# A Fourier filter feeding a snake MLP: the cosine's bias as an immediate, and the transform's pieces placed at other steps

## The chip, the cores and the metric

The kernel runs on one NeuronCore of a Trainium2 chip. The metric is the device time of one execution in microseconds. Five engines run side by side, each with a queue of its own that it works through in order: PE (TensorE, matmuls), ACT (ScalarE), DVE (VectorE), POOL (GpSimd, here only DMA loads that change the type) and SP (SyncE, here all other DMAs after the start).

## The reference

```python
# x (8, 3008, 256), filt_r and filt_i (1505, 256), w_in (256, 2048), w_out (2048, 256), alpha (2048)
X = np.fft.rfft(x, axis=1)
Y = X * (filt_r + 1j * filt_i)[None, :, :]
y = np.fft.irfft(Y, n=3008, axis=1).reshape(8 * 3008, 256)
h = y @ w_in
s = np.sin(alpha * h)
g = h + s * s / (alpha + 1e-09)
out = g @ w_out
```

## The kernel before

**The spectral part.** 3008 = 47 × 64, so each of the 8 batches goes through a transform in two factors and back, in three stages that `spectral(b)` cuts into pieces:

- Stage 1, 8 pieces: a matmul `pa` over the 47 (tile `x`, table `wf_t`), two per piece, evacuated into `t1`; after every second piece a chunk of `t1` is stored to the DRAM buffer `d1`. After the last piece eight loads bring `d1` back in another order as four `t2` tiles, two loads each.
- Stage 2, 13 pieces: piece u does the forward matmul `pb` over the 64 (two of them), its evacuation `xf` by ACT and two products `p` with the filter by DVE, and then, for u − 1, the inverse matmul `pc` (four of them) and its evacuation `g`. Every third one stores `g` to the DRAM buffer `d2` in two DMAs.
- Stage 3, 16 pieces: four small matmuls `pd` over the 47 on a chunk of `d2`, loaded as `t4` (four loads per batch, three buffers), and an evacuation into `y`. Two consecutive pieces fill the two halves of the channels for 376 columns of `y`. `y` holds two batches, even and odd.

`evac` (L135, L137) sends two evacuations in three to ACT and the third to DVE. All matmul results of the spectral part share the two PSUM slots of `fps`; only batch 0's `pb` uses `ops`.

**The MLP.** Two batches are 6016 columns, taken in 12 chunks of at most 512. A chunk is 8 steps. In each step `hidden` runs twice: two matmuls `ph` (L356) into one of the four slots of `hps`, the cosine `cos` by ACT (L359), and `v` = cos − 1 − ph by DVE (L360). With sin² written as a cosine of twice the angle, and alpha folded into the two weight matrices at the start, this is the snake function. Then `project` multiplies 128 columns of the chunk before by half of `w2` (eight matmuls `po`, L371); every fourth step ACT copies the result to `o` (L377) and SP stores it.

**The order.** Batch b's MLP begins at about step 48·b. The list `pending` holds the spectral pieces of batches 1 to 7, and of batch 0 what is left, by the step at which each is due; `plan` gives these steps for each stage. In a step the pieces that are due come after `hidden` and before `project`. This is the order in which the program is written; the tile framework's scheduler then orders every engine's queue by its own estimate of when operands and buffers are ready, with the written order as priority. The trace shows that loads leave earlier than written where their buffer is free.

**The start.** Batch 0's stages run before the MLP. Its loads, the filter's (`filt` into `f_t`, doubled onto the other 64 partitions by `dup_filter`), the inverse table `e_t` (from transposes of `d_t`) and the weights are chained by `after(ins, other)`, which makes a DMA wait for another instruction, and `behind`, which only keeps an order. `marks` keeps the latest instruction of a kind for that: `w_out` is loaded after `marks["t4"]`, and batch 1's `x` after the `marks["t4"]` of its moment.

Of the kernel before, what the change touches and what calls it, by code (L numbers as in the profile page):

```python
# [54 lines left out]
def kernel(  # L55
# [76 lines left out]
    def evac(dst, src, on_act=None):  # L132
        flip[0] = (flip[0] + 1) % 3
        if flip[0] if on_act is None else on_act:
            marks["act"] = nc.scalar.copy(out=dst, in_=src)  # L135
        else:
            marks["dve"] = nc.vector.tensor_copy(out=dst, in_=src)  # L137

    def spectral(b):

        pieces = []
        d1 = dpool.tile([2 * NS, N2, C], FP16, name=f"d1_{b}", tag="d1")
        d2 = dpool.tile([2 * NS, N2, C], FP16, name=f"d2_{b}", tag="d2")
        d1_rows = d1.rearrange("a (h n) c -> (a h) n c", h=2)
        d2_rows = d2.rearrange("a (h n) c -> (a h) n c", h=2)
        st = {}

        def stage1(u):
            ch, half = divmod(u, 2)
            if u == 0:  # L150
                st["x"] = load_x(b)
            if half == 0:
                st["t1"] = t1pool.tile([NK, 8, C], FP16, name=f"t1_{b}_{ch}", tag="t1")
            for i in range(2):
                n0 = 4 * half + 2 * i
                ps = fps.tile([128, 512], FP32, name=f"pa_{b}_{u}_{i}", tag="f")
                marks["pe"] = nc.tensor.matmul(out=ps[0:NK, :], lhsT=wf_t, rhs=st["x"][ch][:, n0:n0 + 2, :],  # L157
                                               start=True, stop=True)
                evac(st["t1"][:, n0:n0 + 2, :], ps[0:NK, :])
            if half == 1:  # L160
                nc.sync.dma_start(out=d1_rows[:, 8 * ch:8 * ch + 8, :], in_=st["t1"])
            if u == 7:
                st["t2"] = []
                for g in range(4):
                    t2 = t2pool.tile([128, 6, C], FP16, name=f"t2_{b}_{g}", tag="t2")
                    for p in range(2):
                        a0 = p * NS + 6 * g
                        eng = nc.scalar if b == 0 and p else nc.sync
                        marks["t2", g] = eng.dma_start(out=t2[64 * p:64 * p + 64, :, :],
                                          in_=d1[a0:a0 + 6, :, :].rearrange("s n c -> n s c"))  # L170
                    st["t2"].append(t2)

        def stage2(u):
            if u < 12:

                ps = (ops if b == 0 else fps).tile([128, 2, C], FP32, name=f"pb_{b}_{u}",
                                                   tag="o" if b == 0 else "f")
                for i in range(2):
                    s = 2 * u + i
                    nc.tensor.matmul(out=ps[:, i, :], lhsT=d_t[:, s, :],  # L180
                                     rhs=st["t2"][s // 6][:, s % 6, :], start=True, stop=True)
                xf = xfpool.tile([128, 2, C], FP16, name=f"xf_{b}_{u}", tag="xf")
                nc.scalar.copy(out=xf, in_=ps)  # L183
                pr = []
                for k in range(2):
                    pt = ppool.tile([128, 2, C], FP16, name=f"p_{b}_{u}_{k}", tag="p")
                    marks["prod", u] = nc.vector.tensor_tensor(out=pt, in0=xf, in1=f_t[k][:, 2 * u:2 * u + 2, :],  # L187
                                                               op=ALU.mult)
                    pr.append(pt)
                st["p", u] = pr  # L190
            if u > 0:
                w = u - 1
                pr = st.pop(("p", w))
                if w % 3 == 0:
                    st["g"] = gpool.tile([128, 6, C], FP16, name=f"g_{b}_{w}", tag="g")
                ps = fps.tile([128, 2, C], FP32, name=f"pc_{b}_{w}", tag="f")
                for i in range(2):
                    for k in range(2):
                        nc.tensor.matmul(out=ps[:, i, :], lhsT=e_t[:, k, 2 * w + i, :],  # L199
                                         rhs=pr[k][:, i, :], start=(k == 0), stop=(k == 1))  # L200
                i0 = 2 * (w % 3)
                evac(st["g"][:, i0:i0 + 2, :], ps, i0 != 2 if b == 0 else None)
                if w % 3 == 2:
                    for p in range(2):
                        a0 = p * NS + 6 * (w // 3)
                        nc.sync.dma_start(out=d2[a0:a0 + 6, :, :].rearrange("s n c -> n s c"),
                                          in_=st["g"][64 * p:64 * p + 64, :, :])

        def stage3(u):
            ch, rest = divmod(u, 4)  # L210
            half, cb = divmod(rest, 2)
            if rest == 0:
                t4 = t4pool.tile([NK, 8, C], FP16, name=f"t4_{b}_{ch}", tag="t4")
                marks["t4"] = nc.sync.dma_start(out=t4, in_=d2_rows[:, 8 * ch:8 * ch + 8, :])
                st["t4"] = t4
            ps = fps.tile([128, 4, 128], FP32, name=f"pd_{b}_{u}", tag="f")
            psv = ps.rearrange("p a b -> p (a b)")[:, 0:4 * NR].rearrange("p (a r) -> p a r", r=NR)
            for i in range(4):
                nc.tensor.matmul(out=psv[:, i, :],  # L219
                                 lhsT=st["t4"][:, 4 * half + i, cb * 128:cb * 128 + 128],  # L220
                                 rhs=wi_t, start=True, stop=True)
# [44 lines left out]

    def dup_filter(g):
        gs = slice(6 * g, 6 * g + 6)
        for k in range(2):
            ins = nc.vector.tensor_copy(out=f_t[k][64:128, gs, :], in_=f_t[k][0:64, gs, :])  # L270
            behind(ins, marks["prod", 3 * g - 2] if g else s1_dve)

    for g in range(4):
        for k, filt in enumerate((filt_r, filt_i)):
            for q in range(2):
                off, step = ((6 * g) * C, C) if q == 0 else ((N1 - 6 * g) * C, -C)
                ins = nc.gpsimd.dma_start(
                    out=f_t[k][32 * q:32 * q + 32, 6 * g:6 * g + 6, :],
                    in_=bass.AP(tensor=filt.tensor, offset=filt.offset + off,
                                ap=[[N1 * C, 32], [step, 6], [1, C]]))  # L280
                if g >= 2:
                    after(ins, marks["t2", g - 2])
    for g in range(3):
        pse = ops.tile([128, 8, 128], FP16, name=f"pse_{g}", tag="o")
        for i in range(8):
# [63 lines left out]
    def hidden(k, jb):  # L349
# [6 lines left out]
            nc.tensor.matmul(out=ps[:, 0:n], lhsT=w1[:, cb, jb * 128:jb * 128 + 128],  # L356
                             rhs=y_cols[:, cb, c0:c0 + n], start=(cb == 0), stop=(cb == 1))
        cs = cospool.tile([128, 512], FP32, name=f"cos_{k}_{jb}", tag="c")
        nc.scalar.activation(out=cs[:, 0:n], in_=ps[:, 0:n], func=AFT.Sin, bias=quarter)  # L359
# [21 lines left out]
    def store(o_blk, pb, col):  # L381

        p = 0
        while p < 128:
# [70 lines left out]
```

## Time and profile before

| | us |
|---|---|
| median of 10 runs | 841.02 (840.12 to 844.12) |
| profiled execution | 840.12, its span 838.3 |
| PE busy | 799.5 (95% of the span) |
| ACT busy | 674.9 (81%) |
| DVE busy | 628.6 (75%) |
| PE clock, mean granted | 0.985 |

Busy time is the time in which an engine has an instruction in work. Matmuls overlap, so a PE that is busy throughout can still stand between two of them. The first 60 us of the span are the start, in which PE is busy for about six tenths and the DMA engines carry the most; after it every slice has PE at nine tenths or more.

### The profile page before, as it was taken

To read this page: it belongs to the slowest core of one execution; us is meant where nothing else is said; L and a number is where in the kernel's file an instruction comes from. 1 tells how busy PE (TensorE), PEld (TensorE's weight loads), DVE (VectorE), ACT (ScalarE), POOL (GpSimd) and SP (SyncE) were. 2 spreads that over 40 slices of the span, in tenths; PEclk is the share of its full clock that TensorE was granted. 3 is DMA by queue.
4 is the path that set the end of the run, shared out by engine and by line. 5 is a ranking of instruction groups with operands and counts; after the bars stand their busy time and mean duration, and the time that the engine had idled before them with its cause. 6 is when DMAs were issued, how large, how long until landed. Compare 5 with 4: busy or idle time off the path is not lost.

```text
span 838.3 us, 16120 instructions
## 1 busy us (share of the span) xinstructions
PE 799.5 (95%) x5793; PEld 543.9 (65%) x5793; DVE 628.6 (75%) x1120; ACT 674.9 (81%) x1200; POOL 28.1 (3%) x55
## 2 busy tenths in 40 slices
PE   5758999999999999999999999999999999999996
PEld 2325676667776676666776677666767677666674
DVE  3658886778877787777877788777877778777772
ACT  4547897888878898888888888888988988788873
POOL 3210000000000000000000000000000000000000
PEclk9959999999999999999999999999999999999998
DMA  9985844285354833367242753447343343421111
GB/s 214 224 246 123 194 95 131 51 177 113 82 135 89 178 84 92 91 137 157 66 130 61 166 135 82 115 91 171 91 97 92 98 113 83 115 57 38 38 39 45
DMA packets 93495, 94.98 MB, mean 113 GB/s; under 512 B 8084, under 2 KB 82852, under 8 KB 93416
## 3 DMA queue, kind: packets, MB, share of 16 engines
q1 hardware_dynamic: 84784, 75.02, 34.6%
q0 software_dynamic: 6704, 18.09, 12.6%
q10 hardware_dynamic: 1928, 0.86, 0.5%
q8 instruction: 45, 0.74, 0.4%
q14 instruction: 34, 0.28, 0.1%
HBM read 58.02 MB, written 49.81 MB: 129 GB/s over the span
## 4 chain that ended last, share of the span: by engine, by line
PE 83%; DMA 6%; DVE 4%; ACT 4%; issue 2%; SPq 0%; ACTq 0%; DVEq 0%; POOLq 0%
PE ph L356 35%; PE po L371 35%; PE pc L199 5%; PE pa L157 4%; DMA t<-d 3%; PE pd L219 2%; PE pb L180 2%; ACT cos L359 2%; DMA w_out<-in_moe_w_out_dram 1%; DVE v L360 1%; DVE p L187 1%; DMA d<-t 1%; DMA d<-g 1%; ACT y L135 1%; DMA x<-in_x_dram 1%
## 5 line engine op out<-in xcount | busy, mean ns | idle before, releaser
L360 DVE SCALAR_TENSOR_TENSOR v<-cos,ph 128x512 f16<-128x512 f32 (+1 forms) x768 | 483.6, 671 | 147.9 <-ACT cos L359 146.9
L359 ACT ACTIVATE cos<-ph,quarter 128x512 f32<-128x512 f32 (+1 forms) x768 | 480.8, 680 | 104.9 <-PE ph L356 103.7
L371 PE MATMUL po<-w,v 128*128 128x256 f16 x3008 | 400.7, 273 | 2.7 <-DVE w L339 2.7
L356 PE MATMUL ph<-y,w 128*128 128x512 f16 (+1 forms) x1536 | 391.8, 377 | 0.2 <-ACT y L135 0.2
L371 PEld LDWEIGHTS <-v 128*128 128x128 f16 x3008 | 288.6, 98 | 79.1 <-issue 7.4
L356 PEld LDWEIGHTS <-w 128*128 128x128 f16 x1536 | 150.7, 98 | 102.8 <-issue 5.5
L187 DVE TENSOR_TENSOR p<-xf,filt 128x512 f16<-128x512 f16 x192 | 71.9, 417 | 5.9 <-ACT xf L183 5.2
L377 ACT COPY o<-po 128x512 f32<-128x512 f32 x96 | 56.5, 589 | 9.8 <-PE po L371 7.4
L183 ACT CAST xf<-pb 128x512 f16<-128x512 f32 x96 | 56.6, 590 | 8.9 <-DMA t<-d 5.5
L199 PE MATMUL pc<-p,e_t 128*128 128x256 f16 x384 | 60.1, 278 | 3.4 <-DVE p L187 2.1
L135 ACT CAST t<-pa 96x512 f16<-96x512 f32 x89 | 50.0, 588 | 15.0 <-PE pa L157 15.0
L219 PEld LDWEIGHTS <-t 96*128 96x128 f16 x512 | 35.7, 99 | 39.3 <-DMA t<-d 12.1
L157 PE MATMUL pa<-x,wf_t 94*96 94x512 f16 x128 | 47.6, 410 | 10.2 <-DMA x<-in_x_dram 6.2
L219 PE MATMUL pd<-wi_t,t 96*128 96x94 f16 x512 | 42.6, 208 | 10.6 <-DMA t<-d 9.9
L199 PEld LDWEIGHTS <-e_t 128*128 128x128 f16 x384 | 37.7, 99 | 16.3 <-issue 7.5
L135 ACT CAST y<-pd 128x376 f16<-128x376 f32 x82 | 38.7, 474 | 11.4 <-PE pd L219 11.4
L180 PE MATMUL pb<-t,d_t 128*128 128x256 f16 x192 | 37.8, 280 | 3.2 <-DMA t<-d 2.4
L135 ACT CAST g<-pc 128x512 f16<-128x512 f32 x64 | 38.7, 605 | 2.2 <-PE pc L199 1.9
L137 DVE CAST y<-pd 128x376 f16<-128x376 f32 x46 | 25.2, 548 | 19.3 <-PE pd L219 19.2
L137 DVE CAST t<-pa 96x512 f16<-96x512 f32 x39 | 26.7, 684 | 17.2 <-PE pa L157 16.6
L180 PEld LDWEIGHTS <-d_t 128*128 128x128 f16 x192 | 18.7, 100 | 24.9 <-DMA t<-d 3.7
L118 POOL DMA_DIRECT2D x<-in_x_dram x32 | 16.6, 522 | 503.6 <-PE pa L157 493.0
(29 smaller groups left out, 86.2 us busy)
## 6 DMA issues: line engine op xcount, KB each, us to landing
d<-t SPq DMA_DIRECT2D x32, 384.0 KB
d<-g SPq DMA_DIRECT2D x64, 192.0 KB
t<-d SPq DMA_DIRECT2D x32, 384.0 KB
x<-in_x_dram POOLq DMA_DIRECT2D x32, 376.0 KB, 7.3
t<-d SPq DMA_DIRECT2D x60, 192.0 KB
out_dram<-o SPq DMA_DIRECT2D x72, 94.0 KB
w_in<-in_moe_w_in_dram POOLq DMA_DIRECT2D x2, 1024.0 KB, 9.1
w_out<-in_moe_w_out_dram POOLq DMA_DIRECT2D x1, 2048.0 KB, 11.9
```

The source lines that it names most:

```text
L135: marks["act"] = nc.scalar.copy(out=dst, in_=src)
L157: marks["pe"] = nc.tensor.matmul(out=ps[0:NK, :], lhsT=wf_t, rhs=st["x"][ch][:, n0:n0 + 2, :], start=True, stop=True)
L180: nc.tensor.matmul(out=ps[:, i, :], lhsT=d_t[:, s, :], rhs=st["t2"][s // 6][:, s % 6, :], start=True, stop=True)
L183: nc.scalar.copy(out=xf, in_=ps)
L187: marks["prod", u] = nc.vector.tensor_tensor(out=pt, in0=xf, in1=f_t[k][:, 2 * u:2 * u + 2, :], op=ALU.mult)
L199: nc.tensor.matmul(out=ps[:, i, :], lhsT=e_t[:, k, 2 * w + i, :], rhs=pr[k][:, i, :], start=(k == 0), stop=(k == 1))
L219: nc.tensor.matmul(out=psv[:, i, :], lhsT=st["t4"][:, 4 * half + i, cb * 128:cb * 128 + 128], rhs=wi_t, start=True, stop=True)
L356: nc.tensor.matmul(out=ps[:, 0:n], lhsT=w1[:, cb, jb * 128:jb * 128 + 128], rhs=y_cols[:, cb, c0:c0 + n], start=(cb == 0), stop=(cb == 1))
L359: nc.scalar.activation(out=cs[:, 0:n], in_=ps[:, 0:n], func=AFT.Sin, bias=quarter)
L360: marks["snake"] = nc.vector.scalar_tensor_tensor(out=v[k][:, jb, 0:n], in0=cs[:, 0:n], scalar=-1.0, in1=ps[:, 0:n], op0=ALU.add, op1=ALU. ...
L371: nc.tensor.matmul(out=pso[k][:, t % 2, :], lhsT=v[k][:, jb, 128 * t:128 * t + 128], rhs=w2[:, jb, :], start=(jb == 0), stop=(jb == 15))
L377: nc.scalar.copy(out=o[:, 0:nb, :], in_=pso[k][:, 0:nb, :])
```

## The change

- `quarter`, a [128,1] tile filled with π/2, is dropped. The cosine takes the number itself as its bias.
- The list of due steps becomes the function `at_step`. With s = 48·b − 4·(b odd), for batches 2 to 7: the loads of `x` at s − 72 (before: with stage 1's first piece, at 48·b − 45), stage 1 at s − 50 to s − 43 (before: 48·b − 45 to − 38), stage 2 at s − 36 to s − 12 in every second step (before: 48·b − 29 to − 16, nearly one per step), stage 3 at s − 6, − 5, − 4, − 3, then − 1, 1, and so on to 21 (before: 48·b − 10, − 9, − 7, − 5, and so on to 19). Batch 1 has stage 1 at 6 to 13 and stage 2 at 21 to 33 (before: 8 to 15 and 23 to 35), and stage 3 by the rule above.
- For batches 2 to 7 `load_x` is a piece of its own, of a stage 0.
- Stage 3 loads `t4` one chunk ahead: chunks 0 and 1 at its first piece, then chunk 2 and chunk 3 at pieces 4 and 8.
- The signs of the second product are placed otherwise: `filt_i` is loaded onto the upper 64 partitions and its negative goes onto the lower ones, and both halves of `e_t[:, 1]` are negated copies. Stage 2 is cut into the functions `forward`, `product` and `inverse`, whose bodies are those of before.

```diff
         def stage1(u):
             ch, half = divmod(u, 2)
-            if u == 0:
+            if u == 0 and b < 2:
                 st["x"] = load_x(b)
...
         def stage2(u):
+
             if u < 12:
...
+                forward(u)
+                st["p", u] = [product(k, u) for k in range(2)]
             if u > 0:
...
+                inverse(u - 1)
+
+        def load_t4(ch):
+            st["t4", ch] = t4pool.tile([NK, 8, C], FP16, name=f"t4_{b}_{ch}", tag="t4")
+            marks["t4"] = nc.sync.dma_start(out=st["t4", ch], in_=d2_rows[:, 8 * ch:8 * ch + 8, :])
 
         def stage3(u):
...
             if rest == 0:
-                t4 = t4pool.tile([NK, 8, C], FP16, name=f"t4_{b}_{ch}", tag="t4")
-                marks["t4"] = nc.sync.dma_start(out=t4, in_=d2_rows[:, 8 * ch:8 * ch + 8, :])
-                st["t4"] = t4
+                for c in ([0, 1] if ch == 0 else [ch + 1] if ch < 3 else []):
+                    load_t4(c)
...
+        if b >= 2:
+            pieces.append((0, lambda: st.update(x=load_x(b))))
         for u in range(8):
             pieces.append((1, lambda u=u: stage1(u)))
...
-    quarter = cpool.tile([128, 1], FP32)
-    nc.vector.memset(quarter, float(np.pi / 2))
...
     def dup_filter(g):
         gs = slice(6 * g, 6 * g + 6)
-        for k in range(2):
-            ins = nc.vector.tensor_copy(out=f_t[k][64:128, gs, :], in_=f_t[k][0:64, gs, :])
+        for ins in (nc.vector.tensor_copy(out=f_t[0][64:128, gs, :], in_=f_t[0][0:64, gs, :]),
+                    nc.vector.tensor_scalar(out=f_t[1][0:64, gs, :], in0=f_t[1][64:128, gs, :],
+                                            scalar1=-1.0, scalar2=None, op0=ALU.mult)):
...
-                    out=f_t[k][32 * q:32 * q + 32, 6 * g:6 * g + 6, :],
+                    out=f_t[k][64 * k + 32 * q:64 * k + 32 * q + 32, 6 * g:6 * g + 6, :],
...
-        nc.vector.tensor_copy(out=e_t[0:64, 1, gs, :], in_=e_t[64:128, 0, gs, :])
-        nc.vector.tensor_scalar(out=e_t[64:128, 1, gs, :], in0=e_t[0:64, 0, gs, :],
-                                scalar1=-1.0, scalar2=None, op0=ALU.mult)
+        for p in range(2):
+            nc.vector.tensor_scalar(out=e_t[64 * p:64 * p + 64, 1, gs, :],
+                                    in0=e_t[64 - 64 * p:128 - 64 * p, 0, gs, :],
+                                    scalar1=-1.0, scalar2=None, op0=ALU.mult)
...
-        nc.scalar.activation(out=cs[:, 0:n], in_=ps[:, 0:n], func=AFT.Sin, bias=quarter)
+        nc.scalar.activation(out=cs[:, 0:n], in_=ps[:, 0:n], func=AFT.Sin, bias=float(np.pi / 2))
...
-    plan = {1: [-45 + i for i in range(8)],
-            2: [-29 + 14 * i / 13 for i in range(13)],
-            3: [-10, -9] + [-7 + 2 * i for i in range(14)]}
+    def at_step(b, stage, i):
+
+        if b == 1 and stage < 3:
+            return 6 + i if stage == 1 else 21 + i
+        return 48 * b - 4 * (b % 2) + (-72 if stage == 0 else -50 + i if stage == 1
+                                       else -36 + 24 * i / 12 if stage == 2
+                                       else -6 + i if i < 4 else -1 + 2 * (i - 4))
+
     pending = [(1 + i % 4 + 8 * (i // 4), 0, piece) for i, (_, piece) in enumerate(first[25:])]
     for b in range(1, B):
-        at = {1: 0, 2: 0, 3: 0}
+        at = {0: 0, 1: 0, 2: 0, 3: 0}
         for stage, piece in spectral(b):
-            at_step = 48 * b + plan[stage][at[stage]]
-            if b == 1 and stage < 3:
-                at_step = 8 + at[stage] if stage == 1 else 23 + at[stage]
+            pending.append((at_step(b, stage, at[stage]), b, piece))
             at[stage] += 1
-            pending.append((at_step, b, piece))
```

More of the change, by code (lines that the diff above doesn't have):

```diff
@@ L171, in stage1, with forward @@
                     st["t2"].append(t2)
+        def forward(u):
+            ps = (ops if b == 0 else fps).tile([128, 2, C], FP32, name=f"pb_{b}_{u}",
+                                               tag="o" if b == 0 else "f")
+            for i in range(2):
+                s = 2 * u + i
+                nc.tensor.matmul(out=ps[:, i, :], lhsT=d_t[:, s, :],
+                                 rhs=st["t2"][s // 6][:, s % 6, :], start=True, stop=True)
+            xf = xfpool.tile([128, 2, C], FP16, name=f"xf_{b}_{u}", tag="xf")
+            nc.scalar.copy(out=xf, in_=ps)
+            st["xf", u] = xf
@@ new lines, in product, with inverse @@
+        def product(k, u):
+            pt = ppool.tile([128, 2, C], FP16, name=f"p_{b}_{u}_{k}", tag="p")
+            marks["prod", u] = nc.vector.tensor_tensor(out=pt, in0=st["xf", u],
+                                                       in1=f_t[k][:, 2 * u:2 * u + 2, :], op=ALU.mult)
+            return pt
+        def inverse(w):
+            pr = st.pop(("p", w))
+            if w % 3 == 0:
+                st["g"] = gpool.tile([128, 6, C], FP16, name=f"g_{b}_{w}", tag="g")
+            ps = fps.tile([128, 2, C], FP32, name=f"pc_{b}_{w}", tag="f")
+            for i in range(2):
+                for k, pt in enumerate(pr):
+                    nc.tensor.matmul(out=ps[:, i, :], lhsT=e_t[:, k, 2 * w + i, :],
+                                     rhs=pt[:, i, :], start=(k == 0), stop=(k == len(pr) - 1))
+            i0 = 2 * (w % 3)
+            evac(st["g"][:, i0:i0 + 2, :], ps, i0 != 2 if b == 0 else None)
+            if w % 3 == 2:
+                for p in range(2):
+                    a0 = p * NS + 6 * (w // 3)
+                    nc.sync.dma_start(out=d2[a0:a0 + 6, :, :].rearrange("s n c -> n s c"),
+                                      in_=st["g"][64 * p:64 * p + 64, :, :])
@@ L173, in stage2 @@
         def stage2(u):
             if u < 12:
[L176 to L182, printed above, removed]
@@ L183, in stage2 @@
-                nc.scalar.copy(out=xf, in_=ps)
-                pr = []
-                for k in range(2):
[L186 to L190, printed above, removed]
-            if u > 0:
[L192 to L207, printed above, removed]
@@ L219, in stage3 @@
                 nc.tensor.matmul(out=psv[:, i, :],
-                                 lhsT=st["t4"][:, 4 * half + i, cb * 128:cb * 128 + 128],
+                                 lhsT=st["t4", ch][:, 4 * half + i, cb * 128:cb * 128 + 128],
                                  rhs=wi_t, start=True, stop=True)
@@ L268, in dup_filter @@
         gs = slice(6 * g, 6 * g + 6)
-        for k in range(2):
-            ins = nc.vector.tensor_copy(out=f_t[k][64:128, gs, :], in_=f_t[k][0:64, gs, :])
+        for ins in (nc.vector.tensor_copy(out=f_t[0][64:128, gs, :], in_=f_t[0][0:64, gs, :]),
+                    nc.vector.tensor_scalar(out=f_t[1][0:64, gs, :], in0=f_t[1][64:128, gs, :],
+                                            scalar1=-1.0, scalar2=None, op0=ALU.mult)):
             behind(ins, marks["prod", 3 * g - 2] if g else s1_dve)
@@ L289 @@
         behind(nc.scalar.mul(e_t[:, 0, gs, :], pse, 0.125), s1_act)
-        nc.vector.tensor_copy(out=e_t[0:64, 1, gs, :], in_=e_t[64:128, 0, gs, :])
-        nc.vector.tensor_scalar(out=e_t[64:128, 1, gs, :], in0=e_t[0:64, 0, gs, :],
-                                scalar1=-1.0, scalar2=None, op0=ALU.mult)
+        for p in range(2):
+            nc.vector.tensor_scalar(out=e_t[64 * p:64 * p + 64, 1, gs, :],
+                                    in0=e_t[64 - 64 * p:128 - 64 * p, 0, gs, :],
+                                    scalar1=-1.0, scalar2=None, op0=ALU.mult)
     ones = cpool.tile([128, 128], FP32)
```

## The prediction

> **What bounds the kernel now.** I read the page first: TensorE (PE) is busy 95% of the span and carries 83% of the chain that ended last. The cosine is the largest ScalarE (ACT) row, and it takes `quarter` as a second operand:
>
> ```profile
> PE 83%; DMA 6%; DVE 4%; ACT 4%; issue 2%; SPq 0%; ACTq 0%; DVEq 0%; POOLq 0%
> ...
> L359 ACT ACTIVATE cos<-ph,quarter 128x512 f32<-128x512 f32 (+1 forms) x768 | 480.8, 680 | 104.9 <-PE ph L356 103.7
> L371 PE MATMUL po<-w,v 128*128 128x256 f16 x3008 | 400.7, 273 | 2.7 <-DVE w L339 2.7
> L356 PE MATMUL ph<-y,w 128*128 128x512 f16 (+1 forms) x1536 | 391.8, 377 | 0.2 <-ACT y L135 0.2
> L377 ACT COPY o<-po 128x512 f32<-128x512 f32 x96 | 56.5, 589 | 9.8 <-PE po L371 7.4
> ```
>
> ACT waits 103.7 us for `ph`, while PE waits only 0.2 us for ACT at the hidden matmuls. So ACT's speed can pay only where PE waits for a PSUM slot that ACT or VectorE (DVE) empties. Busy time hides such waits, because matmul ends are modelled. I therefore took the part at full PE clock from the stage windows:
>
> ```profile
> 72.00:828.00 756.00, 751.51 (x5569) 519.27 (x5568) 588.74 (x1034) 640.55 (x1142) 12.32 (x24) 1.00 0.44 104
> ```
>
> (length; PE, weight loads, DVE, ACT, POOL busy with counts; PE clock, DMA share, GB/s). The same view by line gives the matmuls in it: 1508 `ph` (128 of them 384 wide by the code), 2972 `po`, 109 `pa`, 168 `pb`, 336 `pc`, 476 `pd`.
>
> **What the Trainium skill says.** "TensorE: Matmul & The Clock Gate", section "Wait — 56ns, not 53.3ns?": a warm matmul of N columns starts N/2.4 GHz + about 2.5 ns after the one before. The trace agrees: eight 256-wide `po` run at 0.87 us, 109 ns each. "ScalarE: Activation LUTs", section "What ACT_TABLE_LOAD costs": an ACTIVATE with immediates costs 186 ns + 0.833 ns per element, each [128,1] pointer about 93 ns more, and neighbours overlap by about 93 ns. The trace agrees closely: 680 ns for the cosine against 589 ns for the copy `o` of the same shape, which has no pointer. "VectorE: DVE Perf Modes", section "The perf-mode tier table": tensor_copy and tensor_scalar share a tier. Here the two 64x1024 f16 instructions on `e_t` took 422 and 420 ns.
>
> **The stalls there are to win.** Issue time of that window: 1380×215.8 + 128×162.5 + 2972×109.2 + 109×215.8 + 504×109.2 + 476×42.5 ns (42.5 is the measured pitch of `pd`) = 741.8 us of 756. So PE stands still for 14 us. Going through start-to-start distances and adding each excess over the matmul's own pitch gives 14.0 us: 5.9 before `pa` (stage 1), 4.8 before `pc` (stage 2), 2.3 before `pd` (stage 3), 0.7 before `ph`, 0.3 before `pb`. That is the ceiling: 1.7%. Two typical ones, from the timeline (start, length, engine, line, what):
>
> ```profile
> 367.60 1.26 ACT L359 ACTIVATE cos<-ph,quarter 128x512 f32<-128x512 f32 x2 [0.44 <-PE ph L356]
> ...
> 368.30 0.93 PE L371 MATMUL po<-w,v 128*128 128x256 f16 x7
> ...
> 368.75 0.47 ACT L135 CAST y<-pd 128x376 f16<-128x376 f32 x1
> ...
> 369.28 0.38 PE L157 MATMUL pa<-x,wf_t 94*96 94x512 f16 x1
> ...
> 402.77 0.68 DVE L137 CAST g<-pc 128x512 f16<-128x512 f32 x1
> ...
> 403.01 0.49 PE L371 MATMUL po<-w,v 128*128 128x256 f16 x3
> ...
> 403.50 0.60 PE L199 MATMUL pc<-p,e_t 128*128 128x256 f16 x4
> ```
>
> First: seven `po` from 368.30 are through at 369.07, but `pa` starts at 369.28, when ACT has emptied `y` out of one of the two `fps` slots. ACT came to `y` late because two cosines stood ahead. Second: three `po` end at 403.34, but `pc` waits until 403.50 for DVE's `g`, which stood behind two `v` and two products.
>
> **The change, part by part.**
>
> *Immediate bias.* 768 × about 92 ns = 71 us of ACT time, nearly all off the path. On the path is the queue ahead of an evacuation: two cosines, so 0.18 us sooner, against stalls of 0.05 to 0.3 us before `pa`. I take 3.0 of 5.9 us, with 1 and 5 as bounds: later units inherit the earlier finish, but where more stage-3 units meet stage 1 (below) less is won. The dropped memset is one small instruction at the start, nothing.
>
> *Stage 2 over 24 steps for batches 2 to 7.* The count stays at 13 pieces and 8 stores per batch. A piece every second step gives the two slots 4.1 us instead of 2.4 us, so DVE's `g` is out in time: the 4.1 us before `pc` in these batches go (bounds 2.5 and 4.5). Batch 1 keeps one per step and its 0.7.
>
> *Batch 1 two steps earlier.* Its stage 2 ends 5 steps ahead of stage 3, not 3. A 1.3 us stall before `pd` at 142.9 for `t4` (1.18 us in the waits view) should mostly go: 1.0 (0 to 1.3).
>
> *Stage 3 and `t4`.* Four loads per batch as before. Loading one chunk ahead gains nothing: the scheduler already sends the second and third early (237.19 and 237.56, one step after the first at 235.10). Starting with four units in a row puts 6 of the 8 stage-1 steps of batches 3, 5, 7 beside a stage-3 unit instead of 4: three evacuations through two slots. I charge 0.7 us (0 to 2). Consumers are at least one step later, as before.
>
> *`load_x` as a piece of its own.* POOL carries only loads by then, and each waits for `pa` to free its buffer (4 x tiles; the waits view has 493 us of it). An earlier place in the program changes no issue: 0.
>
> *Filter and `e_t` signs.* Copy becomes tensor_scalar, same counts: 0.
>
> *The price at the start.* `w_out` is released by `marks["t4"]`. Unit 0 now loads two chunks, so the mark is the second one:
>
> ```profile
> 48.28 1.26 SPq L214 DMA_DIRECT2D t<-d  x3
> ...
> 52.90 1.18 POOL L332 DMA_DIRECT2D w_out<-in_moe_w_out_dram  x1 [17.86 <-DMA t<-d]
> ...
> 64.78 1.14 DVE L339 TENSOR_SCALAR w<-w_out,rec_t 128x256 f16<-128x256 f32 x4 [3.35 <-DMA w_out<-in_moe_w_out_dram]
> ...
> 65.19 1.37 PE L371 MATMUL po<-w,v 128*128 128x256 f16 x7 [2.72 <-DVE w L339]
> ```
>
> Three `t4` loads leave SP together; the second lands about 1.6 us after the first (384 KB at the page's best slice, 246 GB/s). `w_out` takes 11.85 us in the chain and PE stands 2.72 us behind it, with DVE's `v` queued behind `w`. So it goes onto the path whole: 1.5 us lost (0 to 3; a further stretch at half clock would be the upper end). Batch 1's x loads now wait for the third `t4`, but POOL sends them after `w_out` anyway.
>
> *The price at the hand-over to stage 2.* From stage 1's last unit to stage 2's first there were 9 steps, now 7. Over 7 steps PE does 7×(4×215.8+8×109.2) + 2×215.8 + 16×42.5 ns = 13.3 us, and the data need: evacuation, `d1` store, `t2` loads.
>
> ```profile
> 470.48 0.60 PE L157 MATMUL pa<-x,wf_t 94*96 94x512 f16 x2
> ...
> 472.92 0.32 SPq L161 DMA_DIRECT2D d<-t  x1
> 474.56 4.29 SPq L389 DMA_DIRECT2D out_dram<-o  x4
> 481.39 5.28 SPq L169 DMA_DIRECT2D t<-d  x8
> ...
> 487.39 0.38 PE L180 MATMUL pb<-t,d_t 128*128 128x256 f16 x2
> ```
>
> That is batch 5: 10.9 us from `pa` to the first `t2` load. Batches 2, 3, 4, 6 took 8.0 to 9.0 us, batch 7 (no x prefetch beside it) 5.3. The first group is two loads; it lands 5.3 us after the first issue in batch 1 (0.65 + 4.64 in the chain). The need is thus 13.3 to 14.3 us, 16.2 in batch 5, against 13.3: 0 to 1 us late in most. By semaphore events other batches land nearer 4.5 us, and evacuations come sooner with the shorter cosine. I charge 2.0 us over six batches (0 to 7). SP has nothing of the batch queued between; output stores wait behind `t2`, with three `o` buffers as cover.
>
> **The sum.** Won: 3.0 + 4.1 + 1.0 = 8.1. Lost: 1.5 + 0.7 + 2.0 = 4.2. Net 3.9 us. The profiled execution took 840.12 us, of which 838.3 are its span; the median of the runs is 841.02, 0.9 above. 840.1 − 3.9 + 0.9 gives **837.0 us**. About 0.2% (1.7 us) is what a measurement of this kernel can tell from no change.
>
> **The rivals.**
>
> *Forecast*, chance 0.52: 833 to 839.2 us.
>
> *All cover holds*, 0.15: `t2` is in time, collisions cost nothing and the start loses nothing or reorders around it. Won 10 to 12, so 829 to 832. For it: batch 7's margin. Against it: the `w_out` chain is visible and has no spare work beside it.
>
> *The saving lands in idle time*, 0.14: ACT's 71 us only lengthen its wait for `ph`, or the immediate isn't decoded as one and the record stays at 680 ns. Stage 2's gain alone (4.1) is eaten by the same losses: 841, within 0.2%. For it: the 103.7 us that ACT already waits. Against it: stalls before `pa` that end with an ACT evacuation.
>
> *`t2` is late*, 0.19, slower: PE is in order, so a late first `t2` stops everything behind `pb`. Against 8.1 won and 2.2 lost elsewhere it decides from 1 us per batch (6 us in all) to even, and from 1.3 us to slower by over 0.2%. At batch 5's 2.9 us in four batches it is 11.6, and the time 847; at 1.4 us in each of six, 843.5. For it: 7 steps against a need of 13.3 to 16.2. Against it: the scheduler places `pb` by its own estimate of the load and can put other matmuls first.
>
> **The numbers.** Faster by over 0.2%: 0.52 + 0.15 = 0.67. Within: 0.14. Slower: 0.19. The range leaves out the best end of the second case and the far end of the last: 830.5 to 843.0 us; the likeliest case's own is 833 to 839.2.
>
> **What would show it.** Right: the cosine near 590 ns, ACT busy near 605 us, no wait of `pc` for DVE's `g` after batch 1, first `po` near 66.7 us, PE gaps before `pb` of at most 1 us. Wrong: gaps before `pb` over 1.3 us in most batches, a `pa` stall sum that hasn't fallen, `w_out` leaving POOL at the old time, or a cosine still at 680 ns.

## The result, and the profile after

The changed kernel is slower: a median of 862.38 us over 9 runs (855.29 to 863.50) against 841.52 us over 31 runs of the kernel before on the same chips, a ratio of 1.0234 on record with a 95% interval of 1.0219 to 1.0250 (the two medians alone give 1.0248). The forecast was 837.0 us, faster. The profiled execution took 862.57 us with a span of 860.7; those of before were 840.12 and 838.3.

The page of the kernel after, first the shares of the chain that ended last, then the groups that answer to those shown of before (busy us, mean ns of one, idle us before them and its releaser):

```profile
PE 74%; DMA 15%; ACT 4%; DVE 3%; issue 2%; SPq 2%; ACTq 0%; DVEq 0%; POOLq 0%
...
L371 ACT ACTIVATE cos<-ph 128x512 f32<-128x512 f32 (+1 forms) x768 | 412.1, 589 | 154.5 <-PE ph L368 153.1
L383 PE MATMUL po<-w,v 128*128 128x256 f16 x3008 | 401.8, 274 | 7.0 <-DVE w L351 7.0
...
L389 ACT COPY o<-po 128x512 f32<-128x512 f32 x96 | 55.3, 576 | 19.7 <-PE po L383 17.7
...
L179 PE MATMUL pb<-t,d_t 128*128 128x256 f16 x192 | 38.4, 284 | 17.1 <-DMA t<-d 16.1
```

Three things can be read here. The cosine is 91 ns shorter, as the Trainium skill, "ScalarE: Activation LUTs", section "What ACT_TABLE_LOAD costs", prices a pointer operand (about 93 ns). Most of those 69 us came back as waiting of ACT: its wait for `ph` rose from 103.7 to 153.1 us, and that of the copy `o` for `po` from 7.4 to 17.7. And DMA went from 6% to 15% of the chain, with a new wait before `pb`. The waits view of the part after batch 1's transform (144 to 828 us, PE alone; us in all, times, longest) shows where:

```profile
PE pb L179 <- DMA t<-d: 13.0, 5, 4.0
PE pd L229 <- DMA t<-d: 2.6, 1, 2.6
PE pa L157 <- ACT y L135: 0.2, 1, 0.2
```

The first matmuls of stage 2 wait for their loads in five batches. The stage windows add what the waits don't show. These are the stretches just around or after three of those waits (length, busy us of PE, weight loads, DVE, ACT and POOL with counts, then the clock, the DMA share and GB/s):

```profile
281.50:288.30 6.80, 5.30 (x24) 3.22 (x25) 2.08 (x4) 2.14 (x4) 0.00 (x0) 0.50 1.14 207
486.30:489.70 3.40, 3.40 (x18) 1.94 (x16) 1.92 (x4) 1.56 (x3) 0.00 (x0) 0.50 1.20 204
595.50:598.90 3.40, 3.40 (x18) 1.87 (x16) 1.30 (x3) 1.43 (x3) 0.00 (x0) 0.51 1.23 218
```

PE runs at half clock there; the `po` in them start 213 ns apart in place of 109.

I sorted the whole difference as the prediction sorted its stalls: by the excess of start-to-start distances of matmuls over their own pitch. The table leaves out excesses under 40 ns (without that limit the kernel before has 5.8 before `pa`, near the 5.9 of the prediction). From the first `ph` of step 8 on, in us; the column "half clock" is the extra time of matmuls at half clock:

| | span | step 8 starts | before pa | pb | pc | pd | ph | half clock |
|---|---|---|---|---|---|---|---|---|
| before | 838.3 | 74.0 | 5.5 | 0.3 | 4.8 | 2.3 | 0.7 | 0 |
| after | 860.7 | 77.1 | 7.1 | 15.1 | 1.3 | 3.3 | 0.2 | 5.9 |

The span grew by 22.4 us: 3.1 at the start, 13.4 in stalls (27.0 against 13.6) and 5.9 in matmuls at half clock. By batch the stalls before `pb` are 1.3 (batch 1), 2.1, 4.2, 1.9, 3.5, 2.2 and, in batch 7, none.

### The profile page after: what moved, and what is told of

It is laid out like the page before. It is cut to its first block, busy times and chain, and to the rows that moved or that the text cites. A ratio compares the mean times of both kernels' runs of the same rounds, so it can differ in the third digit from the quotient of the medians.

```text
span 860.7 us, 16111 instructions
## 1 busy us (share of the span) xinstructions
PE 803.5 (93%) x5793; PEld 545.7 (63%) x5793; DVE 629.3 (73%) x1119; ACT 614.2 (71%) x1200; POOL 28.4 (3%) x55
## 4 chain that ended last, share of the span: by engine, by line
PE 74%; DMA 15%; ACT 4%; DVE 3%; issue 2%; SPq 2%; ACTq 0%; DVEq 0%; POOLq 0%
PE po L383 32%; PE ph L368 30%; DMA d<-t 6%; PE pc L198 5%; DMA t<-d 4%; PE pa L157 3%; PE pb L179 2%; DMA out_dram<-o 2%; ACT cos L371 2%; DMA w_out<-in_moe_w_out_dram 2%; PE pd L229 2%; ACT t L135 1%; SPq L169 1%; DVE v L372 1%; ACT y L135 1%
## 5 line engine op out<-in xcount | busy, mean ns | idle before, releaser
L371 ACT ACTIVATE cos<-ph 128x512 f32<-128x512 f32 (+1 forms) x768 | 412.1, 589 | 154.5 <-PE ph L368 153.1
L383 PEld LDWEIGHTS <-v 128*128 128x128 f16 x3008 | 290.7, 98 | 87.8 <-issue 13.8
L389 ACT COPY o<-po 128x512 f32<-128x512 f32 x96 | 55.3, 576 | 19.7 <-PE po L383 17.7
L229 PEld LDWEIGHTS <-t 96*128 96x128 f16 x512 | 36.3, 100 | 41.1 <-DMA t<-d 12.2
L229 PE MATMUL pd<-wi_t,t 96*128 96x94 f16 x512 | 43.2, 208 | 12.1 <-DMA t<-d 11.6
L135 ACT CAST y<-pd 128x376 f16<-128x376 f32 x86 | 41.2, 481 | 11.9 <-PE pd L229 11.8
L137 DVE CAST t<-pa 96x512 f16<-96x512 f32 x43 | 29.4, 684 | 16.8 <-PE pa L157 16.7
L157 PEld LDWEIGHTS <-wf_t 94*96 94x96 f16 x128 | 16.6, 130 | 18.6 <-issue 10.0
## 6 DMA issues: line engine op xcount, KB each, us to landing
w_out<-in_moe_w_out_dram POOLq DMA_DIRECT2D x1, 2048.0 KB, 15.4
```

The costliest lines, as they stand in the source:

```text
L229: nc.tensor.matmul(out=psv[:, i, :], lhsT=st["t4", ch][:, 4 * half + i, cb * 128:cb * 128 + 128], rhs=wi_t, start=True, stop=True)
L383: nc.tensor.matmul(out=pso[k][:, t % 2, :], lhsT=v[k][:, jb, 128 * t:128 * t + 128], rhs=w2[:, jb, :], start=(jb == 0), stop=(jb == 15))
L389: nc.scalar.copy(out=o[:, 0:nb, :], in_=pso[k][:, 0:nb, :])
```

## What the hand-over looks like

The timeline of the kernel after shows batch 5 (start, length, engine, line, what; in brackets the idle time before and its releaser):

```profile
470.69 0.38 PE L157 MATMUL pa<-x,wf_t 94*96 94x512 f16 x1
471.36 0.51 POOL L118 DMA_DIRECT2D x<-in_x_dram  x1 [3.82 <-PE ph L368]
471.81 0.32 SPq L161 DMA_DIRECT2D d<-t  x1
...
480.64 5.28 SPq L169 DMA_DIRECT2D t<-d  x8
...
485.06 0.38 PE L179 MATMUL pb<-t,d_t 128*128 128x256 f16 x2 [3.28 <-DMA t<-d]
```

The last `pa` is at 470.69 and the store to `d1` leaves 1.1 us later. It takes 8.8 us, so the loads of `t2` can only start at 480.64; the first group needs 4.2 us more. PE stands 3.28 us. In between, POOL issues the next batch's load of `x`, which became free to go when stage 1 released its buffer. The chain of waits of the same kernel gives batch 3, the worst, in pieces (start, length, what):

```profile
269.12 9.62 DMA d<-t
278.74 0.02 issue
278.75 0.60 SPq L169
279.35 0.05 issue
279.40 3.46 DMA t<-d
282.86 0.14 issue
283.00 0.58 PE pb L179 x2
```

The store takes 9.62 of the 13.9 us of this chain. Two theories came out of this. **A:** the hand-over is two steps too short, whatever else changed. **B:** the store is long because the loads of `x` run beside it, so a hand-over of seven steps would do if they didn't. Their rivals were the other parts of the change: the start, the loads of `t4`, the immediate (**C:** ACT's time lands in its own idle time), and the spread of stage 2.

## The experiments

Each edit is against the kernel after unless another is named.

**1. Stage 1 two steps earlier** (nine steps to stage 2, all else kept).

```diff
-        ... -50 + i if stage == 1
+        ... -52 + i if stage == 1
```

> The changed kernel with stage 1 of batches 2 to 7 two steps earlier, so that nine steps lie between its last unit and stage 2's first, as before the change. Theory A (the t2 loads are late by a fixed need of 14 to 17 us from the last pa, and seven steps give 13): two steps are 3.6 us more, so the waits before pb of batches 2 to 6, 13.8 us together, fall to under 2 us, the half-clock stretches that follow them (about 6 us) go, and the time is 843 to 846 us. Rival B (the loads are late because the d1 store itself is held up by the x prefetch and the output stores, which move along with stage 1): the waits only shrink by half and the time is 850 to 856 us. Rival C (the loss lies elsewhere, in the spread stage 2 or the start): 860 us or more.

842.6 us; 1.0012 of before (0.9995 to 1.0029). So two steps at the hand-over are worth 20 us of the 21. Its waits view over the whole span:

```profile
PE pb L179 <- DMA t<-d: 7.7, 3, 5.3
```

The longest, 5.3 us, is batch 0's at the start; batches 1 and 5 have the other 2.3. From step 8 on, the stalls before `pb` fell from 15.1 to 2.8 us and half clock from 5.9 to 1.7. A store took 7.8 to 9.5 us here too: the nine steps cover it, they don't shorten it.

**2. The kernel before, with the hand-over alone shortened.**

```diff
-    plan = {1: [-45 + i for i in range(8)],
+    plan = {1: [-43 + i for i in range(8)],
```

> The kernel before with one number changed: stage 1 of batches 2 to 7 two steps later, so that seven steps lie between its last unit and stage 2's first, as in the changed kernel. Bias pointer, compact stage 2 and loads on demand stay. Theory A (the seven-step hand-over is enough to make the whole loss): waits before pb of 2 to 3 us in batches 2 to 6, some half-clock stretches after the longest, 855 to 862 us. Rival (the change's shorter cosine, earlier stage 3 or spread are needed as well to make the d1 store so slow): waits under 1 us each and 842 to 847 us.

856.26 us; 1.0167 (1.0141 to 1.0194). The old kernel with nothing but a seven-step hand-over loses 14.7 of the 21 us. (Its profiled execution, of 851.9 us, was the shortest of its runs.) Its waits view and a part of its chain:

```profile
PE pb L180 <- DMA t<-d: 10.0, 6, 2.5
```

```profile
284.15 8.66 DMA d<-t
...
292.90 0.60 SPq L169
...
293.55 3.55 DMA t<-d
...
297.24 0.38 PE pb L180 x2
```

One of the six waits, 1.4 us, is batch 0's at the start; the five of batches 2 to 6 are 1.1 to 2.6 us long, where 2 to 3 were expected. The chain is batch 3's: the same three links, with nearly the same lengths, with the old bias, filter and stages 2 and 3. With experiment 1 this shows A from both sides. The waits are shorter than in the kernel after because PE has more to do between the two stages: 13.2 us here, 10.9 to 12.2 there (see the window below).

**3. The loads of `x` kept back until `t2` is loaded.**

```diff
+            if b >= 2:
+                after(ins, marks["t2", 3])
```

> The changed kernel with one wait added: the x loads of batches 2 to 7 start after the batch before has its last t2 load landed, so that no x prefetch runs beside the d1 store and the t2 loads. The seven steps stay. Theory A (a fixed need): as changed, 862 us. Theory B (the x prefetch beside the d1 store is what makes the loads late; batch 7, which has no prefetch beside it, showed no wait): d1 stores take 4 to 5 us instead of 7 to 9.6, the waits before pb of batches 2 to 6 go from 13.8 us to under 3, and with the half-clock stretches gone the time is 843 to 847 us.

842.01 us; 1.0000 (0.9989 to 1.0011): the whole loss is gone at seven steps. The spectral matmuls stand at the same places among `ph` and `po` in PE's queue as in the kernel after, so the edit changes the time of the loads and not the order of PE. From 76 us on, its waits view for PE has no line for `pb` and begins with `pd`; below it is batch 5 in its timeline:

```profile
PE pd L231 <- DMA t<-d: 2.8, 1, 2.8
```

```profile
458.99 0.38 PE L159 MATMUL pa<-x,wf_t 94*96 94x512 f16 x1
460.11 0.32 SPq L163 DMA_DIRECT2D d<-t  x1
463.62 5.28 SPq L171 DMA_DIRECT2D t<-d  x8
...
469.91 0.38 PE L181 MATMUL pb<-t,d_t 128*128 128x256 f16 x2
```

The store now takes 3.5 us where it took 8.8 (3.0 in batches 2, 3, 4 and 6), `t2` lands 8.3 to 9.0 us after the last `pa`, and `pb` comes without a wait 10.9 to 12.2 us after it. So B is right as well, and it names the cause of the length: A and B are two ends of one inequality, and either end mends it.

**4. The immediate alone, in the kernel before.**

```diff
-    quarter = cpool.tile([128, 1], FP32)
-    nc.vector.memset(quarter, float(np.pi / 2))
...
-        nc.scalar.activation(..., bias=quarter)
+        nc.scalar.activation(..., bias=float(np.pi / 2))
```

> The kernel before with one edit of the change alone: the bias as an immediate, quarter dropped. Theory A (the bias is a gain and the loss is all in the schedule): cosine near 589 ns, waits before pa fall from 5.5 to about 2.5 us and nothing else moves, 836 to 839 us. Rival B (the shorter cosine lets the scheduler order the queues otherwise and part of the loss comes with it, at the start above all): 843 to 848 us. Rival C (ACT's time is all off the path): 841 us.

841.24 us; 0.9993 (0.9983 to 1.0003): no gain that can be measured, as rival C has it. The page says where the time went:

```profile
L357 ACT ACTIVATE cos<-ph 128x512 f32<-128x512 f32 (+1 forms) x768 | 411.7, 590 | 153.2 <-PE ph L354 151.2
```

Again ACT waits instead: of the 69 us, 48 are in the wait for `ph` (103.7 before). The stalls before `pa` didn't fall: 6.0 us against 5.5. The stall that the prediction used as its example is still there in the timeline of this kernel:

```profile
363.23 0.82 PE L369 MATMUL po<-w,v 128*128 128x256 f16 x6
363.58 0.48 ACT L135 CAST y<-pd 128x376 f16<-128x376 f32 x1
364.11 0.38 PE L157 MATMUL pa<-x,wf_t 94*96 94x512 f16 x1
```

Six `po` are through 0.65 us after 363.23, at 363.88, and `pa` starts at 364.11: 0.23 us, against 0.21 before. ACT finishes `y` earlier, and `pa` has been put one `po` earlier (six stand ahead of it, seven before). In the queue of PE as the two programs have it, 30 of the 128 `pa` stand at least one `po` or `ph` earlier than before, 11 later, and 92 of the 384 `pc` stand one place earlier. The reading is that the scheduler, which orders by its own estimates, moved the consumer up with the cheaper producer; the moved places are shown, its reason is argued.

**5. The pointer put back, on top of experiment 3.**

```diff
-        nc.scalar.activation(..., bias=float(np.pi / 2))
+        nc.scalar.activation(..., bias=quarter)
```

> The changed kernel with the x prefetch behind the t2 loads (842.0 us), but with the bias as the [128,1] operand again. Theory A (ACT's time is off the path in this schedule too, and the scheduler places pa by its own estimate of the evacuation either way): cosine near 680 ns and 841 to 843 us, no difference that can be measured. Rival (the shorter cosine is what carries the denser stage 3 beside stage 1): waits before pa rise from 7 to 10 us or more and the time is 845 to 848 us.

840.44 us; 0.9987 (0.9978 to 0.9995). The page has the longer cosine again:

```profile
L375 ACT ACTIVATE cos<-ph,quarter 128x512 f32<-128x512 f32 (+1 forms) x768 | 480.7, 679 | 101.3 <-PE ph L372 98.2
```

Experiment 3 with the immediate is at 1.0000: the *longer* cosine is no slower, by the medians 1.6 us faster, though the two intervals overlap a little. Before `pa` PE stands 5.2 us with the pointer and 7.1 with the immediate. Here too about a third of the `pa` have another place in the two queues. That the other order is what makes the 1.9 us is argued from this and not shown by a run of its own.

**6. `w_out` released by the first load of `t4`.**

```diff
+            marks.setdefault("t4_first", marks["t4"])
...
-          marks["t4"])
+          marks["t4_first"])
```

> The changed kernel with w_out released by the first t4 load again, not by the second. Theory A (the second t4 load releases w_out 1.5 us later and the start loses that): w_out leaves about 1.5 us earlier and the time falls by 1.5 to 2 us, to 860 to 861 us. Rival B (w_out took 15.4 us instead of 11.9 because it shares the queues with the fourth t4 load and x, whatever releases it): first po is at most 0.5 us earlier and the time stays at 862 us. Rival C (the longer stand of PE, 7.0 us against 2.7, is all from the release): 4 us less, 858 us.

861.98 us; 1.0238 (1.0210 to 1.0265), so not to be told from the kernel after at 1.0234. Yet in the profiled executions the start differs. First the kernel after, then this one, in the timeline:

```profile
69.33 2.19 DVE L351 TENSOR_SCALAR w<-w_out,rec_t 128x256 f16<-128x256 f32 x8 [7.29 <-DMA w_out<-in_moe_w_out_dram]
...
69.74 1.06 PE L383 MATMUL po<-w,v 128*128 128x256 f16 x4 [7.05 <-DVE w L351]
```

```profile
65.49 1.14 DVE L352 TENSOR_SCALAR w<-w_out,rec_t 128x256 f16<-128x256 f32 x4 [3.43 <-DMA w_out<-in_moe_w_out_dram]
...
65.90 1.39 PE L384 MATMUL po<-w,v 128*128 128x256 f16 x7 [3.19 <-DVE w L352]
```

The two `w_out` loads left within 0.6 us of each other (53.90 and 53.29) and took 15.4 and 12.2 us. In the ten other kernels it took 11.9 to 13.5, four of them with the release of the kernel after, so 15.4 us are not what this start takes as a rule. The runs of both kernels spread by 4 to 8 us, so one execution settles little. What the later release costs is estimated from all the kernels further down; what made this one load slow stays open.

**7. Each chunk of `t4` loaded at its own piece, on top of experiment 3.**

```diff
-                for c in ([0, 1] if ch == 0 else [ch + 1] if ch < 3 else []):
+                for c in [ch]:
```

> The changed kernel with the x prefetch behind the t2 loads (as in the run before with that edit, 842.0 us) and with each t4 chunk loaded by the unit that uses it, as before the change; so the first t4 load releases w_out again. Theory A (a second load beside the first makes the first land later, 6.1 to 6.3 us in batch 1 against 4.3, and w_out leaves later): the wait before pd in batch 1 falls from 2.8 us to about 1, the half-clock stretch after it (1.7 us) goes, and the start gains 1.5: 837.5 to 839 us. Rival (the scheduler sends the loads together whatever the program says, and w_out's landing is the queues' affair): 841 to 842 us.

840.52 us; 0.9985 (0.9976 to 0.9994), between what theory and rival had expected, and by the medians 1.5 us below experiment 3, though the two intervals overlap. The wait before `pd` of batch 1 stays (2.78 us with loading ahead, 2.57 without), and so does a half-clock stretch behind it. So loading ahead is not the cause of that wait: in both kernels three loads of `t4` leave together, 5.2 us after the last two stores of `g` went out. That it releases `w_out` later may be the 1.5 us.

**8. Batch 1's stage 2 two steps earlier still, on top of 7.**

```diff
-            return 6 + i if stage == 1 else 21 + i
+            return 6 + i if stage == 1 else 19 + i
```

> The run with t4 on demand and x behind t2, and batch 1's stage 2 two steps earlier still (steps 19 to 31), since its t2 data are there by 97 us where step 21 comes at 100. Theory A (batch 1's stage 3 waits for the chain from stage 2's last unit to t4, which then has two steps more): no wait before pd in batch 1, 0.5 to 1.5 us less than that run, 836.5 to 838 us. Rival (the earlier stage 2 meets more of stage 3 of batch 0 and the start, and t2 is late there): a wait before pb at step 19 of 1 us or more and no gain.

838.04 us; 0.9957 (0.9941 to 0.9972). Its waits view from 76 us on begins:

```profile
PE pb L181 <- DMA t<-d: 0.8, 1, 0.8
```

The wait before `pd` is gone, with it the half-clock stretch behind it; 0.79 us before `pb` comes in its place, the hand-over of this one batch.

**9. That, with the pointer.** The edits of 7, 8 and 5 together.

> The fastest run so far (x behind t2, t4 on demand, batch 1's stage 2 at steps 19 to 31; 838.0 us) with the bias as the [128,1] operand again. Theory A (the 69 us of ACT time are off the path and the pa waits depend on where the scheduler puts pa, 5.2 us with the pointer against 7.1 with the immediate): 836 to 838 us, equal or up to 2 us faster. Rival (the immediate does pay once nothing else stalls): 839.5 us or more.

836.47 us; 0.9943 (0.9930 to 0.9957), the fastest: 5 us below the kernel before. Against experiment 8 it is 1.6 us, the same step as from 3 to 5, and again the intervals overlap. In the profiled executions the part after the start of step 8 is 1.9 us shorter with the pointer in the first pair and 1.8 in the second, with 2.1 and 1.9 us less of stalls. So two pairs agree that the immediate costs a little in this schedule; one pair alone would not show it. The fastest kernel keeps the new places of stages 2 and 3 and leaves the immediate out.

**10. Stage 2 compact again, on top of experiment 3.**

```diff
-        ... -36 + 24 * i / 12 if stage == 2
+        ... -36 + 14 * i / 13 if stage == 2
```

> The changed kernel with the x prefetch behind the t2 loads (842.0 us), but with stage 2 of batches 2 to 7 compact as before the change: 13 pieces over 14 steps, from the same first step on. Theory A (the spread takes away the waits before pc for DVE's g, 4.8 us before and 1.4 with the spread): the waits before pc are back at 4 to 5 us and the time is 844.5 to 846 us. Rival (the spread is worth nothing on the clock, as the bias was): 841 to 843 us.

849.14 us; 1.0091 (1.0074 to 1.0108), dearer than expected. `pc` stands 3.4 us (1.4 with the spread) and `pd` 8.4 (3.5). At these places a compact stage 2 runs beside the end of stage 3 of the batch before, and the three evacuations of `fps` meet. From its timeline:

```profile
290.12 0.60 PE L385 MATMUL po<-w,v 128*128 128x256 f16 x4
290.20 0.59 ACT L184 CAST xf<-pb 128x512 f16<-128x512 f32 x1
290.85 0.33 PE L231 MATMUL pd<-wi_t,t 96*128 96x94 f16 x4
```

The `po` are through at 290.56; `pd` waits until ACT has finished `xf` at 290.79. The 7 us are thus not the spread's worth in the schedule before, where that meeting didn't exist. For the spread alone the better number is `pc` in the table: 4.8 us before, 1.3 after.

## Why the prediction was wrong, step by step

**Where it failed: the price at the hand-over.** The charge was 2.0 us with an upper bound of 7; it was 13.8 us of stalls before `pb` in batches 2 to 6, and the half clock around or behind three of them another 5.9. Three terms of that sum were off, all to the same side (the total of the prediction is off by rounding alone, 837.1 for 837.0):

- *The window.* Seven steps of PE were put at 13.3 us, with eight `po` in each. In the kernel before with seven steps (experiment 2) that is right: without the wait, 13.2 us lie between the last `pa` and the first `pb`. In the new places it is less, as the experiment without a wait shows: 12.1 to 12.2 us in batches 2, 4 and 6, and 10.9 to 11.5 in 3, 5 and 7. Counting the matmuls in PE's queue gives the reason. The last `pa` stands behind five to eight `po` of its own step, where it stood ahead of all of them before. And in batches 3, 5 and 7 one of the seven steps projects nothing: these steps now fall on the 384-wide chunk, whose six projections are spread over eight steps. So 49 or 50 of the 56 `po` are left in the even batches and 40 to 43 in the odd ones, and 12 of the 16 `pd`. Batches 3 and 5 have the two longest waits, 4.0 and 3.28 us.
- *The need.* It was taken from the kernel before, 13.3 to 14.3 us. There the last store took 5.7 to 8.4 us, mean 6.9, with the loads of `x` beside it. In the kernel after it took 6.1 to 9.6, mean 8.5, and the data landed 14.0 to 15.2 us after the last `pa`. So 2 to 4 us late in a batch, where 0 to 1 was forecast. Batch 7, with no such load, stood out in the prediction too (5.3 us against 8 to 11), but I read it as a margin of one batch and not as the price of the loads in the five others. (The 10.9 us of batch 5 there count from the first of two `pa`; from the last, as in the other batches, it is 10.7.)
- *The clock.* No cost of standing still was in the sum beyond the standing itself; I had named it for the start only. The Trainium skill, "TensorE: Matmul & The Clock Gate", section "What's actually happening", says that the clock falls to half after an idle window of about 3.4 us, and that the window is free-running. The second half is borne out by the clock records of these traces. In the kernel after, half-clock stretches begin at 46.00, 66.48, 281.52, 486.32, 595.54 and 854.96 us: 6, 63, 60, 32 and 76 times 3.413 us apart, and those that end inside the span last one, two or three times as long. So they stand on a fixed grid; in the eleven other traces they do too, each on a grid of its own. The first half doesn't hold here as it stands: much less than a whole idle period was enough. What sorts the waits is how much of one falls into a *single* period of that grid (a wait is the idle time that the trace shows before a matmul):

| wait of PE | us | longest part in one period | half clock |
|---|---|---|---|
| experiment 6, `pb` of batch 5 | 2.15 | 1.30 | no |
| after, `pd` of batch 1 | 2.56 | 1.54 | no |
| after, `pb` of batch 2 | 1.95 | 1.78 | no |
| after, `pb` of batch 6 | 2.04 | 2.04 | yes |
| after, `pb` of batch 5 | 3.28 | 2.15 | yes |
| experiment 7, `pd` of batch 1 | 2.57 | 2.26 | yes |
| after, `pb` of batch 3 | 4.00 | 2.51 | yes |

All 29 waits of over 0.9 us after the start, in the twelve traces, sort in this way: 17 with up to 1.78 us in one period brought no half clock, 12 with 2.04 or more did: the period that followed ran at half clock. Where such a wait reached 1.2 or 1.5 us into that period (batch 3 in experiment 6 and in the kernel after), the one behind it did so too. No wait had between 1.78 and 2.04 us in one period, and PE was at work in the rest of these periods. Where a wait falls on the grid is chance, so of two waits of 2.56 and 2.57 us one was followed by half clock and the other not.

The rival "`t2` is late" had the mechanism, the place and the sign, and its point of decision (1.3 us per batch) was passed in every batch from 2 to 6. Its price of 843.5 to 847 was too small: the stalls came to 13.8 us instead of 8.4 to 11.6, half clock added 5.9, and of the 8.1 us that it took as won only the 3.5 of stage 2 were. The counter-argument, that the scheduler can put other matmuls first, isn't borne out: `pb` stands seven steps behind stage 1 in PE's queue in all these batches, and PE stood still before it. Two of the signs named for being wrong came true: gaps before `pb` of 1.7 to 4.0 us in batches 2 to 6, and a `pa` stall sum that hadn't fallen.

**The immediate: 3.0 us forecast, none found** (experiments 4 and 5). The instruction is as short as forecast (589 ns; ACT's busy time fell to 614 us, where about 605 was expected), and the two cosines did stand ahead of `y` in the queue before. What failed is the step from "ACT is done 0.18 us sooner" to "PE stands 0.18 us less": the order of PE came out otherwise with the shorter cosine, and the consumer in the example moved with its producer. That the scheduler's estimates are the reason is argued. The rival "lands in idle time" was right on this part.

**The spread of stage 2: 4.1 forecast, 3.5 found.** The stalls before `pc` went from 4.8 to 1.3 us. This step was right, in mechanism and size.

**Batch 1 two steps earlier: 1.0 forecast, a loss found.** Its stall before `pd` rose from 1.2 to 2.6 us, and `pb` waited 1.15 us. From the start of the last evacuation `g` to the moment when PE had come to `pd` there were 9.5 us instead of 8.2, but the way through `d2` took 12.1 us instead of 9.3: three loads of `t4` left together and the first landed 6.1 us later, where two had left and the first took 4.3. Five steps between the stages were still too few; two more (experiment 8) took the wait away.

**Stage 3 and the collisions: 0.7 charged.** With the pointer, the new schedule stands 5.2 us before `pa` (experiment 5) against 5.5 in the kernel before: the collisions cost nothing there. With the immediate it is 7.1 against 6.0 (experiment 4), a loss of 1.1 us and within the bounds of 0 to 2. That loading ahead gains nothing was right (experiment 7).

**The start: 1.5 charged.** 3.1 in the profiled execution of the kernel after, with its one slow load of `w_out`; not measurable in the medians (experiment 6). Taken over the profiled executions, step 8 starts at 75.3 to 77.1 us in the five kernels with the new places that release `w_out` by the second load of `t4` (mean 76.2), and at 73.7 to 75.5 in the four that release it by the first (mean 74.8). That is 1.4 us, as an estimate from nine single executions: the charge was about right.

**`load_x` as a piece, and the signs:** nothing in any run speaks against zero, but no run tests them alone. Yet the reason given for `load_x`, that its place in the program doesn't set when it is issued, was also the hint: its issue is set by stage 1 freeing its buffers, and so falls beside the store by construction.

Open: why the store is longer in the kernel after (mean 8.5 us) and in experiments 1 and 2 (8.5 in both) than in the kernel before (6.9), with the same loads of `x` beside it in all four. In the kernel after, the store leaves 0.4 to 0.7 us after the last load of `x` is issued and takes 8.8 to 9.6 us, except in batch 4, where it leaves 2.9 us after it and takes 6.1; in the kernel before it is 1.1 to 1.5 us and 5.7 to 8.4. That fits, but in experiment 2 the distance is 1.1 to 2.0 us and the store takes 7.9 to 8.9 all the same. The place of stage 1 against the output stores, which come every fourth step, differs too; no run separates the two.

## What to carry to other kernels

When a piece is moved, measure the slack of each round trip through DRAM in the case with the traffic and in the one without, since the difference is the price of the traffic; here holding back one prefetch was worth as much as two steps of cover. Take the window from the queue in its new order, from the last producer to the first consumer, and not from a count of equal steps. Reckon with a half-clock stretch behind any wait of about 2 us and more: here one of a single period cost 1.5 to 1.7 us. A shorter instruction off the critical path gave nothing by itself here, and in the new schedule it seems to have cost a little.

## What the hardware showed that I had not expected

- A store of 384 KB from SBUF to DRAM took 3.0 us alone and 6.1 to 9.6 us beside the casting loads of `x` (376 KB each, through POOL's queue): two to three times as long. The DMA engines weren't full meanwhile: in batch 5 of the kernel after their mean busy share was 0.65 over the 8.8 us, at 154 GB/s, where they reach 218 at other moments.
- PE's clock was at half for 3.4 us after a wait of only 2.04 us, and for 6.8 us around one of 4.0 us. In each of the twelve traces the half-clock stretches stand on a grid of 3.413 us; after the start, a period with 2.04 us or more of one wait was followed by one at half clock, and a period with 1.78 or less was not.
- Standing still costs PE more than the gap: the stalls of the hand-over were 13.8 us, and the slow matmuls behind them 5.9 us, or 43% on top.
